# Releasing loads behind TensorE's steps and queueing one-hot rows by step, in windowed attention with a sticky mixture of experts

## The chip, the cores and the metric

The kernel runs on 1 core of one Trainium2 chip. The metric is the device time of one execution in microseconds (us). A profile is one further execution, taken with the hardware profiler; its trace gives every instruction a start and a duration. TensorE (PE) multiplies matrices and transposes, VectorE (DVE) and ScalarE (ACT) work on PSUM and SBUF, GpSimd (Pool) does masked copies and indirect gathers, and SyncE (SP) issues most of the transfers. PE, SP, ACT and Pool each follow their own program in order.

## The reference

Eight batches of eight heads: 512 local and 32 global tokens, head width 64, all in float32. A local token attends to the 32 global tokens and to local tokens at most 32 away; a global token attends to all 544. The result, one row of 512 numbers per token, goes through a mixture of 8 experts of which each token uses one. The choice is sticky:

```
s_l = concat([q_l @ k_g, where(|i - j| <= 32, q_l @ k_l, -1e9)]) / 8 ; out_l = softmax(s_l) @ [v_g, v_l]
out_g = softmax(q_g @ [k_g, k_l] / 8) @ [v_g, v_l]
x = [out_g, out_l] with the heads side by side            # (8, 544, 512)
logits = x @ w_gate ; gate = sigmoid(x @ w_local)
for each batch, for s in order:
    e = argmax(logits[s]) if s == 0 or gate[s] < 0.5 else the expert of token s - 1
    out[s] = softmax(logits[s])[e] * (relu(x[s] @ w1[e]) @ w2[e])     # w1: 512x1024, w2: 1024x512
```

## The kernel before

**Attention.** Class Attn works in 48 steps (`run`, from L427). A batch has six: l0, l1, g0, l2, g1, l3. An l step is a pair of heads of local queries, a g step the global queries of two pairs. Step s makes the scores of unit s and, for the unit of two steps before, the transposes and the products with v. On PE an l step is: transposes of the older unit (L264, or L332 after a global unit), the mask written into two PSUM score banks (L236), a piece of transposing finished rows for the router (L356), 32 score matmuls in two banks of 16 (L247), and 64 small products with v (L280, or 48 at L343 for a global unit). A g step has its scores at L300. DVE takes maxima and subtracts them bank by bank (L252, L254), ACT takes exponentials (L258) and copies transposes out of PSUM (L266, L333).

**Operands.** One q and k load per pair (`load`, L178, 528 KB) fills one of four buffers, `raw`; one v load per pair (`loadv`, L188, 1040 KB) fills one of four `v` buffers; a batch has one load of the global queries (L182). All are issued by SP in program order, each l step asking for q and k two pairs ahead and then for v one pair ahead. An issue waits only for its buffer to be free. Pool copies q and k into the layout of the scores (`prep`, L191: `qbd` in two selects, `kx` in four; two buffers of each), one pair ahead of the scores.

**Router.** The routing of finished batches is written as generators (`gens`). `drip` takes a few of their instructions at a time and puts them between DVE's maximum and subtraction, so they run amid attention: keys (L741 in `keys`), probabilities (L769 in `probs`), then `f4`, which stores the batch's rows to a scratch table in DRAM: the local rows from ACT's queue (L420, 1056 KB), the global ones in four transfers from SP (L424), and their numbers from ACT (L425). After the fifth batch `stage_a` ranks the tokens of the first five batches, and `low` makes 21 one-hot tiles of 128x128 (L916), one Pool instruction each, in a run of 3 tiles per turn of the generator. `pick` then has 21 matmuls of these tiles with `oe` on PE (L1013), whose sums give the rows that the first three blocks of the mixture gather. Nothing else uses these tiles until later lists are made.

**Mixture.** Weights come in pieces of 512 KB (L1154); ACT rounds each into a high part (L1164), and DVE, or Pool for the first two, subtracts it to get a low part (L1174). Three products of high and low parts stand for one in float32. `mm1` (L1265) multiplies a block of 256 tokens by w1, ACT and DVE make the high and low parts of the result (L1267, L1268), and `mm2` (L1276) multiplies by w2. PSUM has eight banks, `ps[0]` to `ps[7]`: attention's score banks are `ps[0]` to `ps[2]`, and the router's transposes (L356) use `ps[3]`. The mixture's ring `ph` of results of `mm1` starts with `ps[2]`, then `ps[3]`. Its first block begins before attention has ended: the last two units' transposes and products, and the last batches' routing, are put between its matmuls (`tail`, `hook`).

Of the kernel before, what the change touches and what calls it, by code (L numbers as in the profile page):

```python
# [18 lines left out]
P = 128  # L19
# [19 lines left out]
NX = 3  # L39
LISTS = "lists"  # L40
# [58 lines left out]
class Attn:  # L99
    def __init__(self, tc, cst, tl, at1, at2, raw, ps, qk, qg, vw, xs):  # L100
# [29 lines left out]
        self.cur = {}  # L130
        self.gens = []
# [40 lines left out]
    def load(self, b, pr):  # L172
        nc = self.nc
        if pr == 0:
            self.cur[b] = {"v": []}
        c = self.cur[b]
        t = c[("qk", pr)] = self.ld()
        nc.sync.dma_start(t, self.qk[b, pr])  # L178
# [5 lines left out]
    def loadv(self, b, pr):  # L184
        nc = self.nc
        v = self.v()
        self.cur[b]["v"].append(v)
        nc.sync.dma_start(v.rearrange("p w c -> p (w c)"), self.vw[b, pr])  # L188
# [49 lines left out]
    def l_s(self, st, hb):  # L238
# [4 lines left out]
        for t in range(4):  # L243
            for t2 in range(2):
                w = 8 * hb + 2 * t + t2
                f = 32 * (3 * (w // 2) + w % 2)
                nc.tensor.matmul(sp[64 * t2:64 * t2 + 64, t], qbd[:, w], kf[:, f:f + P], start=False, stop=True, skip_group_check=True)  # L247
# [12 lines left out]
    def l_t(self, st, hb):  # L260
        nc = self.nc
        tp = self.bank(self.ps_t)
        for i in range(4):
            nc.tensor.transpose(tp[:, i], st["pe"][:, 4 * hb + i], self.cst.idf)  # L264
# [61 lines left out]
    def g_t(self, st):  # L326
        nc = self.nc
        pt = st["pt"] = self.ptg()
        for c0 in (0, 3):
            tp = self.bank(self.ps_t)  # L330
            for i in range(3):
                nc.tensor.transpose(tp[:, i], st["pg"][:, c0 + i], self.cst.idf)  # L332
# [80 lines left out]
    def f4(self, b, rt):  # L413
# [6 lines left out]
        nc.scalar.dma_start(self.xs[r0:r0 + 4 * P].rearrange("(t p) r -> p t r", p=P), xa)  # L420
# [4 lines left out]
        nc.scalar.dma_start(xsg[:, DM:ROW], rt.gx[rq])  # L425

    def run(self, rt, moe):  # L427
# [29 lines left out]
        for s in range(n):  # L457
# [4 lines left out]
            sg = st is not None and not sl  # L462
            if nl:
                if npr + 2 < len(pairs):
                    b, i = pairs[npr + 2]["u"]
                    self.load(b, i)
                    if i == 0:
                        self.load_g(b)
                if npr + 1 < len(pairs):
                    self.loadv(*pairs[npr + 1]["u"])  # L470
                npr += 1
                if npr < len(pairs):
                    self.prep(pairs[npr])
            if sl:
                self.l_t(st, 0)
                self.l_t(st, 1)
            if sg:
                self.g_t(st)
            if nl:
# [5 lines left out]
            if nl:  # L485
                self.l_s(nx, 0)
                self.l_max(nx, 0)
# [111 lines left out]
class Route:  # L599
# [186 lines left out]
    def stage_a(self, pk, po):  # L786
# [11 lines left out]
        for c0 in range(0, CA, 3):  # L798
            yield from self.low(c0, min(c0 + 3, CA), True)
# [194 lines left out]
    def pick(self, cid, phi, o2, c0, c1, i0, groups, po, wait=2):  # L994
# [14 lines left out]
        yield from lag(wait)  # L1009
        yield PSUM  # L1010
# [74 lines left out]
class Moe:  # L1085
    def __init__(self, tc, cst, rt, xs, buf, raw, ps, w1, w2, out):
# [14 lines left out]
        self.ph, self.py, self.xtp = Ring(ps[2:4]), Ring(ps[0:2]), Ring(ps[4:6])  # L1101
# [68 lines left out]
    def flush(self):  # L1170
        nc = self.nc
        while self.pend:
            pool, raw, hi, lo = self.pend.pop(0)
            (nc.gpsimd if pool else nc.vector).tensor_tensor(out=lo, in0=raw, in1=hi.bitcast(F32), op=ALU.subtract)  # L1174
# [326 lines left out]
def kernel(ctx: ExitStack, tc: tile.TileContext, qk, qg, vw, wgl, wgg, w1, w2, out):  # L1501
# [23 lines left out]
    at.at1, at.at2 = s1, s2  # L1525
    at.run(rt, moe)
# [57 lines left out]
```

## Time and profile before

| | before |
|---|---|
| median of 3 runs | 692.18 us (690.45 to 694.25) |
| the profiled execution, its own time | 690.5 us |
| its span | 688.8 us |
| mean granted TensorE clock | 0.984 |
| PE busy | 659.1 us, 96% |
| DVE busy | 425.9 us, 62% |
| ACT busy | 343.0 us, 50% |
| Pool busy | 212.0 us, 31% |
| scores of local pairs (L247) | 1024 matmuls, 65.9 us |
| moved by the DMA engines | 151.45 MB, 220 GB/s |

The span is the time from the first to the last instruction in the trace; the execution's own time is 1.7 us longer. Attention takes about the first 240 us, the mixture the rest. In rows of the trace "out<-in" names the tiles that an instruction writes and reads, xN counts instructions, and what stands in brackets behind a row is the idle time of the engine before it and what ended it. In groups of waits the columns are the total in us, how many times, and the longest.

### The profile page before, as it was taken

The page shows a single profiled execution, that of the slowest core. Times are in us where ns is not written, and L with a number is a line of the kernel's source. Part 1 is how long each engine was busy: PE and PEld are TensorE (multiplying, and loading weights), DVE is VectorE, ACT ScalarE, POOL GpSimd, SP SyncE. Part 2 cuts the span into 40 slices and gives each one's busy share as a digit, 9 for nine tenths or more (in the row PEclk, how much of TensorE's full clock was granted, in tenths as well). Part 3 has the DMA queues.
Part 4 walks back from the last instruction along what each step waited for, and adds up shares of the span by engine and source line. Part 5 has one row for each costly group of instructions (what it writes and reads, how often), then busy time and mean ns, then how long its engine had stood idle before and what let it go on. Part 6 is the DMA issues. An engine that isn't in the chain of part 4 may idle for free.

```text
span 688.8 us, 18451 instructions
## 1 busy us (share of the span) xinstructions
PE 659.1 (96%) x7253; PEld 566.6 (82%) x7253; DVE 425.9 (62%) x1050; ACT 343.0 (50%) x614; POOL 212.0 (31%) x342
## 2 busy tenths in 40 slices
PE   8999999999979799998998999999999999999995
PEld 7788788877767788887887988889898889888994
DVE  7878787777877777994517636325354516255573
ACT  4565565664646474653326635344444325255563
POOL 7734434343674211132022403040403020133023
PEclk9999999999999899999998999999999999999998
DMA  8957977979576486878319547347466417265673
GB/s 334 362 210 258 335 257 276 346 279 332 177 285 227 158 309 234 264 247 277 125 60 320 196 161 244 101 130 230 149 213 194 146 57 230 68 227 177 226 272 103
DMA packets 43012, 151.45 MB, mean 220 GB/s; under 512 B 7965, under 2 KB 9245, under 8 KB 38688
## 3 DMA queue, kind: packets, MB, share of 16 engines
q1 hardware_dynamic: 30928, 118.25, 49.4%
q0 software_dynamic: 6960, 21.90, 9.6%
q10 hardware_dynamic: 4896, 8.80, 3.5%
q8 instruction: 78, 1.28, 0.8%
q14 instruction: 150, 1.23, 0.6%
HBM read 130.55 MB, written 19.69 MB: 218 GB/s over the span
## 4 chain that ended last, share of the span: by engine, by line
PE 80%; DVE 10%; POOL 4%; issue 4%; ACT 1%; POOLq 0%; ACTq 0%; DVEq 0%
PE ps L1276 27%; PE ps L1265 25%; PE ps L247 7%; PE ps L264 4%; PE ps L280 3%; PE ps L1219 3%; PE ps L300 2%; POOL o L916 2%; PE ps L356 2%; PE ps L343 2%; DVE wp L1174 2%; PE ps L332 1%; DVE wq L1174 1%; PE ps L371 1%; PE ps L236 1%
## 5 line engine op out<-in xcount | busy, mean ns | idle before, releaser
L1282 POOL DMA_INDIRECT out_dram<-y,tk x39 | 42.9, 1100 | 315.1 <-ACT y L1281 232.7
L1276 PE MATMUL ps<-wp,wq 128*128 128x512 f32 x504 | 129.5, 404 | 1.0 <-ACT wq L1379 1.0
L1276 PEld LDWEIGHTS ps<-wp,wq 128*128 128x128 f32 x504 | 94.1, 192 | 21.3 <-ACT wq L1379 1.3
L1265 PE MATMUL ps<-wp,wp 128*128 128x256 f32 (+5 forms) x672 | 109.3, 322 | 0.3 <-issue 0.3
L1265 PEld LDWEIGHTS ps<-wp,wp 128*128 128x128 f32 x672 | 103.6, 188 | 5.3 <-issue 0.4
L1268 DVE SCALAR_TENSOR_TENSOR wq<-ps,wq 128x256 fp32r<-128x256 f32 (+5 forms) x80 | 41.7, 525 | 73.8 <-ACT wq L1267 66.4
L1267 ACT ACTIVATE wq<-ps 128x256 fp32r<-128x256 f32 (+5 forms) x80 | 37.3, 469 | 79.1 <-PE ps L1265 69.4
L1222 DVE TENSOR_TENSOR wp<-ps,wp 128x512 fp32r<-128x512 f32 x40 | 27.6, 691 | 78.3 <-ACT wp L1221 78.2
L191 POOL TENSOR_SCALAR_AFFINE_SELECT qbd<-raw 64x512 f32<-64x512 f32 x62 | 44.4, 715 | 89.1 <-PE ps L247 69.7
L247 PE MATMUL ps<-kx,qbd 128*64 128x128 f32 x1024 | 65.9, 280 | 3.9 <-POOL kx L191 3.5
L247 PEld LDWEIGHTS ps<-kx,qbd 128*64 128x64 f32 x1024 | 56.6, 139 | 11.8 <-POOL kx L191 6.7
L1281 ACT ACTIVATE y<-ps,pp 128x512 f32<-128x512 f32 x39 | 26.9, 689 | 77.7 <-PE ps L1276 70.7
L252 DVE TENSOR_REDUCE mx<-ps 128x4 f32<-128x512 f32 x64 | 43.8, 685 | 32.0 <-PE ps L247 32.0
L258 ACT ACTIVATE pe<-pe 128x512 f32<-128x512 f32 x64 | 40.8, 638 | 43.3 <-DVE pe L254 43.3
L1174 DVE TENSOR_TENSOR wp<-raw,wp 128x1024 fp32r<-128x1024 f32 x47 | 56.9, 1217 | 2.9 <-ACT wp L1164 2.8
L1205 POOL DMA_INDIRECT xa<-xs,idx x42 | 52.3, 1245 | 16.3 <-issue 10.0
L1164 ACT CAST wp<-raw 128x1024 fp32r<-128x1024 f32 x49 | 50.9, 1047 | 2.7 <-DVE f L930 1.5
L1221 ACT CAST wp<-ps 128x512 fp32r<-128x512 f32 x40 | 23.4, 588 | 53.2 <-PE ps L1219 53.2
L254 DVE TENSOR_TENSOR pe<-ps,mx 128x512 f32<-128x512 f32 x64 | 43.9, 686 | 1.0
L191 POOL TENSOR_SCALAR_AFFINE_SELECT kx<-raw 128x384 f32<-128x384 f32 (+3 forms) x127 | 43.2, 373 | 2.9 <-DMA raw<-in_qk_dram 0.8
L266 ACT COPY pt<-ps 128x512 f32<-128x512 f32 x64 | 34.7, 600 | 9.8 <-PE ps L264 9.1
L280 PEld LDWEIGHTS ps<-v,pt 128*32 128x32 f32 x2048 | 32.0, 110 | 9.2 <-issue 6.5
(280 smaller groups left out, 1182.5 us busy)
## 6 DMA issues: line engine op xcount, KB each, us to landing
raw<-in_w_dram SPq DMA_DIRECT2D x78, 512.0 KB, 4.3
v<-in_vw_dram SPq DMA_DIRECT2D x32, 1040.0 KB, 7.9
raw<-in_qk_dram SPq DMA_DIRECT2D x32, 528.0 KB, 7.5
xa<-in_w_dram SPq DMA_DIRECT2D x26, 512.0 KB, 4.7
xT<-in_w_dram SPq DMA_DIRECT2D x20, 512.0 KB, 5.3
xs<-xa ACTq DMA_DIRECT2D x8, 1056.0 KB, 8.6
qgb<-in_qg_dram SPq DMA_DIRECT2D x8, 128.0 KB, 5.0
xa<-xs,idx POOLq DMA_INDIRECT x42, 4.9
```

What stands on the lines that cost most here:

```text
L191: self.nc.gpsimd.affine_select(out=out, in_=in_, pattern=pat, compare_op=ALU.is_ge, fill=0.0, base=0, channel_multiplier=0)
L247: nc.tensor.matmul(sp[64 * t2:64 * t2 + 64, t], qbd[:, w], kf[:, f:f + P], start=False, stop=True, skip_group_check=True)
L252: nc.vector.tensor_reduce(out=mx, in_=st["sps"][hb], axis=AX.X, op=ALU.max)
L254: nc.vector.tensor_tensor(out=st["pe"][:, 4 * hb:4 * hb + 4], in0=st["sps"][hb], in1=mx.broadcast_to([P, 4, P]), op=ALU.subtract)
L280: nc.tensor.matmul(o[32 * w4:32 * w4 + 32, g, h], pt[:, 2 * g + w4 // 2, w4 % 2, h, :], v[:, w, h * (D + 1):(h + 1) * (D + 1)], start=True ...
L1164: nc.scalar.copy(out=hi, in_=raw)
L1174: (nc.gpsimd if pool else nc.vector).tensor_tensor(out=lo, in0=raw, in1=hi.bitcast(F32), op=ALU.subtract)
L1205: self.nc.gpsimd.indirect_dma_start(out=self.xr[j] if k == "early" else self.xr4[:, j], out_offset=None, in_=src, in_offset=bass.IndirectO ...
L1265: nc.tensor.matmul(ph, a[:, dc, fs], b_[:, dc, n0:n1], start=(n == 0), stop=(n == 11))
L1268: nc.vector.scalar_tensor_tensor(out=hl[:, fc, n0:n1], in0=ph, scalar=0.0, in1=hh[:, fc, n0:n1].bitcast(F32), op0=ALU.max, op1=ALU.subtract)
L1276: nc.tensor.matmul(py, a[:, fc, js], b_[:, fs], start=(fc == 0 and k == 0), stop=(fc == 7 and k == 2))
L1282: sc = nc.gpsimd.indirect_dma_start(out=self.out, out_offset=bass.IndirectOffsetOnAxis(ap=self.g[1][:, j:j + 1], axis=0), in_=y, in_offset ...
```

## The change

There are five parts.

1. `get` issues q, k and v loads with a dependency besides the buffer's. An l step emits its v load behind its transposes, and it depends on the last of them; q and k (and behind them the global queries, which have no such dependency) are emitted behind the first score bank and depend on its last matmul, except in step 0. SP's order turns from q and k, then v, to v, then q and k.
2. Of the 21 one-hot tiles the first 6 are made by DVE, in two instructions of 3 tiles; the other 15 are put into a list `pq` of five turns of 3 Pool instructions. An l step takes one turn, behind its `prep`; a g step takes two. `pick` goes on only once the list is empty.
3. The last batch's stores of local rows and of its numbers are issued by SP.
4. The ring `ph` starts with `ps[3]`, then `ps[2]`.
5. Pool's split of a weight piece is four instructions of 256 columns.

The core of the diff:

```
+CD = 6
...
+        self.gate = self.last = None
+        self.pq = []
...
         t = c[("qk", pr)] = self.ld()
-        nc.sync.dma_start(t, self.qk[b, pr])
+        self.get(t, self.qk[b, pr])
...
-        nc.sync.dma_start(v.rearrange("p w c -> p (w c)"), self.vw[b, pr])
+        self.get(v.rearrange("p w c -> p (w c)"), self.vw[b, pr])
+
+    def get(self, out, in_):
+        d = self.nc.sync.dma_start(out, in_)
+        if self.gate is not None:
+            self.tc.add_manual_dep(d.ins, self.gate.ins.name, mybir.DependencyInfo(mybir.DependencyClass.Sync, mybir.DependencyReason.DATA), reason="pace")
...
-        nc.scalar.dma_start(self.xs[r0:r0 + 4 * P].rearrange("(t p) r -> p t r", p=P), xa)
+        q = nc.scalar if b < B - 1 else nc.sync
+        q.dma_start(self.xs[r0:r0 + 4 * P].rearrange("(t p) r -> p t r", p=P), xa)
...
-        nc.scalar.dma_start(xsg[:, DM:ROW], rt.gx[rq])
+        q.dma_start(xsg[:, DM:ROW], rt.gx[rq])
...
+            ahead = pairs[npr + 1:npr + 3] if nl else []
             if nl:
-                if npr + 2 < len(pairs):
-                    b, i = pairs[npr + 2]["u"]
-                    self.load(b, i)
-                    if i == 0:
-                        self.load_g(b)
-                if npr + 1 < len(pairs):
-                    self.loadv(*pairs[npr + 1]["u"])
                 npr += 1
                 if npr < len(pairs):
                     self.prep(pairs[npr])
+            for _ in range(2 - nl):
+                if self.pq:
+                    self.pq.pop(0)()
...
+            self.gate = self.last
+            if ahead:
+                self.loadv(*ahead[0]["u"])
...
                 self.l_s(nx, 0)
+                self.gate = self.last if s > 0 else None
+                if len(ahead) > 1:
+                    b, i = ahead[1]["u"]
+                    self.load(b, i)
+                    if i == 0:
+                        self.load_g(b)
                 self.l_max(nx, 0)
...
-        for c0 in range(0, CA, 3):
-            yield from self.low(c0, min(c0 + 3, CA), True)
+        for c0 in range(0, CD, 3):
+            yield from self.low(c0, c0 + 3, False)
+        for c0 in range(CD, CA, 3):
+            self.pq.append(lambda c0=c0: all_(self.low(c0, min(c0 + 3, CA), True)))
...
+        while self.pq:
+            yield
         yield PSUM
         lp = po()
...
-        self.ph, self.py, self.xtp = Ring(ps[2:4]), Ring(ps[0:2]), Ring(ps[4:6])
+        self.ph, self.py, self.xtp = Ring([ps[3], ps[2]]), Ring(ps[0:2]), Ring(ps[4:6])
...
-            (nc.gpsimd if pool else nc.vector).tensor_tensor(out=lo, in0=raw, in1=hi.bitcast(F32), op=ALU.subtract)
+            m = 4 if pool else 1
+            for k in range(m):
+                f = slice(1024 // m * k, 1024 // m * (k + 1))
+                (nc.gpsimd if pool else nc.vector).tensor_tensor(out=lo[:, f], in0=raw[:, f], in1=hi[:, f].bitcast(F32), op=ALU.subtract)
```

Line numbers move: L178 and L188 become L192 (both in `get`), L191 L197, L247 L253, L264 L270, L420 L427, L424 L431, L741 L754, L916 L931, L1013 L1030, L1174 L1194, L1265 L1285.

On PE, from the second score bank of the last batch's l1 (kx_147, qbd_145), before; `ps` are PSUM banks, `o` the one-hot tiles, `pe` the exponentials:

```order
L247 MATMUL ps_63<-kx_147,qbd_145 64x128 x8
L280 MATMUL ps_70<-v_136,pt_142 32x65 x16
L280 MATMUL ps_69<-v_136,pt_143 32x65 x16
L264 MATMUL ps_68<-idf,pe_138 128x128 x4
L264 MATMUL ps_67<-idf,pe_138 128x128 x4
L363 MATMUL ps_66<-idf,xg_111 128x128
L300 MATMUL ps_64<-raw_77,qgb_153 64x256
L300 MATMUL ps_64<-raw_78,qgb_153 64x256
L300 MATMUL ps_65<-raw_77,qgb_153 64x288
L300 MATMUL ps_65<-raw_78,qgb_153 64x288
L1013 LDWEIGHTS o_290
L1013 MATMUL ps_70<-oe,o_290 128x12
```

The same place after, from the mask of that unit; the one-hot matmuls' first, and their last with what follows:

```order
L242 MATMUL ps_65<-mask,idb 128x4x2x32
L242 LDWEIGHTS idb
L242 MATMUL ps_63<-mask,idb 128x4x2x32
L362 MATMUL ps_66<-idf,xa_108 128x128 x4
L253 MATMUL ps_65<-kx_147,qbd_145 64x128 x8
L1030 LDWEIGHTS o_290
...
L1030 MATMUL ps_70<-oe,o_290 128x12
L253 MATMUL ps_63<-kx_147,qbd_145 64x128 x8
L286 MATMUL ps_69<-v_136,pt_142 32x65 x16
L286 MATMUL ps_70<-v_136,pt_143 32x65 x16
```

The 21 matmuls moved from behind the scores of g0 to between the two score banks of l1. The last six of them (tiles 15 to 20) wait for Pool's last turn.

On Pool, the one-hot tiles amid the preparations, before: raw_80 is the last pair of the seventh batch, raw_77 and raw_78 the first two of the last.

```order
L916 TENSOR_SCALAR o_290<-io_261,plo 128x128 x12
L191 AFFINE_SELECT qbd_145<-raw_80 64x16x32 x2
L191 AFFINE_SELECT kx_147<-raw_80 128x128
L191 AFFINE_SELECT kx_147<-raw_80 128x6x64
L191 AFFINE_SELECT kx_147<-raw_80 128x32
L191 AFFINE_SELECT kx_147<-raw_80 128x7x32
L916 TENSOR_SCALAR o_290<-io_261,plo 128x128 x9
L191 AFFINE_SELECT qbd_144<-raw_77 64x16x32 x2
```

After, from the first pair of the last batch to its third (raw_79):

```order
L931 TENSOR_SCALAR o_290<-io_261,plo 128x128 x6
L197 AFFINE_SELECT qbd_144<-raw_77 64x16x32 x2
...
L931 TENSOR_SCALAR o_290<-io_261,plo 128x128 x3
L197 AFFINE_SELECT qbd_145<-raw_78 64x16x32 x2
...
L931 TENSOR_SCALAR o_290<-io_261,plo 128x128 x3
L197 AFFINE_SELECT qbd_144<-raw_79 64x16x32 x2
...
L931 TENSOR_SCALAR o_290<-io_261,plo 128x128 x3
```

Nine tiles stood ahead of the first pair's preparation; six do now, and the last three turns stand ahead of the second pair, ahead of the third, and behind the third.

On SP, the loads of the end of one batch and the start of the next in mid-attention (raw_79 and raw_80 are third and fourth pairs, raw_77 a first), before, with the semaphores that each waits for:

```order
L178 DMA raw_79<-in_qk_dram 128x1056 [waits DMAHW1_49,Pool_49]
L188 DMA v_134<-in_vw_dram 128x2080 [waits DMAHW3_49,PE_49]
L178 DMA raw_80<-in_qk_dram 128x1056 [waits DMAHW5_49,Pool_49]
L188 DMA v_135<-in_vw_dram 128x2080 [waits DMAHW6_49,PE_49]
L178 DMA raw_77<-in_qk_dram 128x1056 [waits DMAHW7_49,PE_49,Pool_49]
```

After:

```order
L192 DMA v_134<-in_vw_dram 128x2080 [waits DMAHW2_49,PE_49]
L192 DMA raw_79<-in_qk_dram 128x1056 [waits DMAHW4_49,PE_49,Pool_49]
L192 DMA v_135<-in_vw_dram 128x2080 [waits DMAHW5_49,PE_49]
L192 DMA raw_80<-in_qk_dram 128x1056 [waits DMAHW6_49,PE_49,Pool_49]
L192 DMA v_136<-in_vw_dram 128x2080 [waits DMAHW7_49,PE_49]
```

Each v load stands ahead of its step's q and k, and every q and k load waits for PE.

More of the change, by code (lines that the diff above doesn't have):

```diff
@@ L172, in load @@
     def load(self, b, pr):
-        nc = self.nc
         if pr == 0:
@@ L184, in loadv @@
     def loadv(self, b, pr):
-        nc = self.nc
         v = self.v()
         self.cur[b]["v"].append(v)
-        nc.sync.dma_start(v.rearrange("p w c -> p (w c)"), self.vw[b, pr])
+        self.get(v.rearrange("p w c -> p (w c)"), self.vw[b, pr])
[3 more added lines that the diff above has]
+            self.tc.add_manual_dep(d.ins, self.gate.ins.name, mybir.DependencyInfo(mybir.DependencyClass.Sync, mybir.DependencyReason.DATA), reason="pace")
     def cp(self, out, in_, pat):
@@ L246, in l_s @@
                 f = 32 * (3 * (w // 2) + w % 2)
-                nc.tensor.matmul(sp[64 * t2:64 * t2 + 64, t], qbd[:, w], kf[:, f:f + P], start=False, stop=True, skip_group_check=True)
+                self.last = nc.tensor.matmul(sp[64 * t2:64 * t2 + 64, t], qbd[:, w], kf[:, f:f + P], start=False, stop=True, skip_group_check=True)
     def l_max(self, st, hb):
@@ L263, in l_t @@
         for i in range(4):
-            nc.tensor.transpose(tp[:, i], st["pe"][:, 4 * hb + i], self.cst.idf)
+            self.last = nc.tensor.transpose(tp[:, i], st["pe"][:, 4 * hb + i], self.cst.idf)
         pt = self.pt()
@@ L331, in g_t @@
             for i in range(3):
-                nc.tensor.transpose(tp[:, i], st["pg"][:, c0 + i], self.cst.idf)
+                self.last = nc.tensor.transpose(tp[:, i], st["pg"][:, c0 + i], self.cst.idf)
             nc.scalar.copy(out=pt[:, c0:c0 + 3], in_=tp[:, 0:3])
@@ L1525 @@
     at.at1, at.at2 = s1, s2
+    rt.pq = at.pq
     at.run(rt, moe)
```

## The prediction

> **What bounds the kernel now.** I read the page's busy times, stretches of 20 to 26 us (start and end; length; busy time and instructions of PE, PEld, DVE, ACT, POOL; granted clock; DMA share; GB/s), then what PE waited for in the first 345 us.
>
> ```profile
> span 688.8 us, 18451 instructions
> 10.00:30.00 20.00, 19.06 (x413) 15.43 (x411) 16.69 (x58) 12.44 (x29) 13.74 (x44) 1.00 1.01 396
> 90.00:110.00 20.00, 20.00 (x429) 16.30 (x427) 16.36 (x59) 12.61 (x32) 7.21 (x17) 1.00 0.82 287
> 190.00:210.00 20.00, 16.16 (x377) 13.66 (x366) 16.16 (x62) 8.75 (x20) 12.48 (x25) 0.91 0.82 295
> 210.00:236.00 26.00, 22.06 (x387) 19.16 (x386) 20.17 (x60) 13.42 (x30) 10.64 (x12) 0.87 0.51 176
> PE ps L1265 <- DVE pe L254: 3.7, 1, 3.7
> PE ps L247 <- POOL kx L191: 3.5, 2, 2.9
> PE ps L343 <- issue: 2.8, 3, 1.2
> PE ps L264 <- issue: 1.3, 2, 0.8
> PE ps L356 <- issue: 0.7, 1, 0.7
> PE ps L247 <- issue: 0.3, 1, 0.3
> ```
>
> A wait row gives the total, how often, and the longest. TensorE sets the time: busy 20.00 of 20 us in mid-attention. It loses time in two places, before 210 us (16.16 of 20, clock 0.91) and before 236 us (22.06 of 26, clock 0.87), by one wait of 3.5 us for Pool and one of 3.7 for DVE. Another 2.8 + 1.3 + 0.7 + 0.3 = 5.1 us is idle with no releaser. The change touches all three.
>
> **1. The Pool stall goes (-5.4).** Pool's and PE's rows in order of time, and the stretch after the stall:
>
> ```profile
> 187.97 5.24 POOL L916 TENSOR_SCALAR o<-io,plo 128x128 bf16<-128x128 bf16 x9
> 193.16 1.49 POOL L191 TENSOR_SCALAR_AFFINE_SELECT qbd<-raw 64x512 f32<-64x512 f32 x2
> 194.73 1.50 POOL L191 TENSOR_SCALAR_AFFINE_SELECT kx<-raw 128x128 f32<-128x128 f32 x4
> 195.24 0.44 PE L247 MATMUL ps<-kx,qbd 128*64 128x128 f32 x4 [2.94 <-POOL kx L191]
> 196.28 3.25 PE L247 MATMUL ps<-kx,qbd 128*64 128x128 f32 x28 [0.60 <-POOL kx L191]
> 196.08:199.49 3.41, 3.21 (x32) 2.88 (x33) 1.62 (x4) 0.00 (x0) 2.89 (x7) 0.50 0.87 334
> 201.96 1.97 PE L247 MATMUL ps<-kx,qbd 128*64 128x128 f32 x32
> ```
>
> Nine one-hot rows (0.58 us each) stand ahead of the last batch's first qbd and kx; PE waits 2.94 + 0.60, and the clock is then 0.50 for 3.41 us, in which half is lost: 1.7. With three rows a step this preparation starts over 5 us earlier. I count 2.94 + 0.60 + 1.7 and 0.2 of pipeline gap: -5.4.
>
> **2. A new wait stands 1.3 steps later (+7.1).** The one-hot matmuls (L1013, L1030 after) come only once Pool's queue list is empty, which puts them between the two score banks of the last batch's second pair. Matmuls 16 to 21 read Pool's last three rows, and those stand behind the preparation of the third pair, whose q and k load is now held until the first pair's first bank.
>
> ```profile
> 78.04 1.90 PE ps L247 x32
> 86.85 1.90 PE ps L247 x32
> 76.36 1.02 PE ps L264 x8
> DMA to landing us min/median/max: 4.8/7.9/11.4
> DMA to landing us min/median/max: 3.6/7.5/12.2
> 207.18 0.67 PE L1013 MATMUL ps<-oe,o 128*128 128x12 bf16 x21
> 193.14 0.37 ACTq L420 DMA_DIRECT2D xs<-xa  x1
> ```
>
> The first two rows are score starts two steps apart: 8.81, so 4.41 a step. The landings are v's, then q and k's. Without stall 1 PE reaches the new place about 197.5 (201.96, plus 0.95 for half of those 32 matmuls, less 5.4). Pool's line, in before's time: the second pair's load opens behind the fourth pair's first bank of the batch ahead, near 188.6 (two steps of 4.41 before 201.96 less stall 1, plus 0.95), lands 4.5 later (0.9 above the fastest), and its preparation takes 3.0 by rows 193.16 and 194.73, to 196.1; three rows take 1.75, to 197.85; the third pair's preparation 3.0 again, to 200.85; three rows more, to 202.6. So PE waits 5.1 even if the third load is no limit. With that load opened a step later, at 193.0, and landing after 7.5 (the median; the store of the activations, issued at 193.14 before, shares the DMA engines) it is 193.0 + 7.5 + 3.0 + 1.75 = 205.25: a wait of 7.75. I take 5.5, nearer the lower end, because with loads spread out a landing nearer the fastest is likely. After the shorter wait above the clock cost 1.7, and it could fall through two such stretches: 0.5 to 3.4, taken 1.9. The place that L1013 left, where DVE's sums held PE for some 0.3, gives that back. Together +7.1 (5.3 to 10.9). Behind the waiting matmul stand the second bank, and with it DVE's subtract and ACT's exponentials.
>
> **3. Loads held back (+0.7, and +1.0 at the start).** By the chain rows a third pair's scores follow the first's by 8.81. v's gate opens after the transposes (76.36 + 1.02 = 77.38); the fastest v landing puts it at 82.18, q and k's 528 KB behind it take 1.37 at 396 GB/s, to 83.55, preparation 3.0, to 86.55; PE wants it at 86.85. So 0.3 us are to spare once in each of 7 batches, and the median landings would miss it.
>
> ```profile
> SPq L188 <- PE ps L343: 103.5, 14, 9.4
> 11.02 1.50 POOL L191 TENSOR_SCALAR_AFFINE_SELECT qbd<-raw 64x512 f32<-64x512 f32 x2 [1.21 <-DVE mx L252]
> 15.39 1.97 PE L247 MATMUL ps<-kx,qbd 128*64 128x128 f32 x32
> ```
>
> SyncE already waited 103.5 us for PE to free v buffers, so the queue was paced before; the hold binds q and k, whose early issue goes. I take +0.7: most fit, some miss by little. Below it is 0; above it 7.7, worked out under the rival Slower. At the start v's second load now goes ahead of q and k of the third pair, in a stretch at 396 GB/s: 1040 KB take 2.7 us. The preparation at 11.02 ends 3.0 later, 1.4 ahead of the scores at 15.39; 2.7 later it would be 1.3 late: +1.0, since it did not start at its landing but at DVE's release (0 to 1.3).
>
> **4. End of attention (-3.9).** DVE, Pool, PE and ACT in order of time, the 0.50 stretch, and the same DVE operation elsewhere:
>
> ```profile
> 222.53 3.03 DVE L741 TENSOR_TENSOR leq<-leq,ro 128x40 f32<-128x40 f32 x1
> 256.39 0.20 DVE L741 TENSOR_TENSOR leq<-leq,ro 128x40 f32<-128x40 f32 x1
> 223.14 2.36 POOL L1174 TENSOR_TENSOR wp<-raw,wp 128x1024 fp32r<-128x1024 f32 x1
> 229.49 2.06 DVE L769 TENSOR_SCALAR lsu<-lsu 128x5 f32<-128x5 f32 x1
> 191.17 0.32 DVE L769 TENSOR_SCALAR lsu<-lsu 128x5 f32<-128x5 f32 x1
> 229.16 2.36 POOL L1174 TENSOR_TENSOR wp<-raw,wp 128x1024 fp32r<-128x1024 f32 x1 [3.67 <-ACT wp L1164]
> 227.54 2.07 PE L1265 MATMUL ps<-xh,wp 128*128 128x256 f32 x8 [3.74 <-DVE pe L254]
> 226.80:233.62 6.82, 6.08 (x28) 6.08 (x29) 5.31 (x20) 1.90 (x5) 2.36 (x1) 0.50 0.32 106
> 232.42 0.43 ACTq L420 DMA_DIRECT2D xs<-xa  x1
> 233.45 0.38 ACT L1267 ACTIVATE hh<-ps 128x256 fp32r<-128x256 f32 x1 [4.23 <-DVE gx L783]
> 234.26 0.93 PE L343 MATMUL ps<-v,ptg 128*32 128x65 f32 x48 [0.20 <-ACT ptg L333]
> ```
>
> L741 takes 0.20 alone and 3.03 when it overlaps Pool's split, ending with it (225.56, 225.50); L769 likewise ends at 231.55 with the second (231.52), but took 0.32 amid Pool's stream of 0.58 us rows. In pieces of 0.6 the two lose at most one piece each: 3.03 - 0.6 + 2.06 - 0.6 = 3.9 comes out of DVE's line. The other score bank frees PE from L254, so the 3.74 stall goes. What is late next is ACT: the sixth batch's stores (L420) wait for DVE, and hh and the global transposes' copy stand behind them, releasing PE at 234.26. That chain moves up by DVE's 3.9: PE at 230.4. I take -3.9; at best 3.74 + 1.9 = -5.6, if full clock holds; if pieces follow without a gap, 0.
>
> The Trainium skill, "SBUF — State Buffer", section "Who interferes with whom", says that a DVE instruction with two SBUF inputs and a Pool one exclude each other, the later waiting for the whole instruction. L741 agrees (3.03 against 0.20). Taken strictly it speaks against this change: the one-hot tiles moved to DVE have two SBUF inputs and meet Pool's selects, and each would wait for one select and then take its own time, 1.1 together; were none of it covered, the sum would be 2.2 worse and 0.5 in place of -1.7. Here it is covered, as point 5 works out from DVE's idle share.
>
> **5. The rest (-1.2).** The unexplained 5.1 us depend on where instruction fetches fall among the queues' traffic; spread loads may ease them: -1.0 (-5.1 to +3, as others may appear). The last stores leave ACT: two issues of 0.4 us, -0.2 (-1.5 to 0). Two one-hot operations on DVE:
>
> ```profile
> 288.07 2.02 DVE L919 TENSOR_TENSOR o<-io,plo 128x640 bf16<-128x640 bf16 x3
> ```
>
> Three of five tiles cost 0.67, so one of three tiles 0.4, inside DVE's idle 3.6 of 20 us: 0 (to +0.8).
>
> **The sum.** -5.4 + 7.1 + 0.7 + 1.0 - 3.9 - 1.2 = -1.7. The profiled execution takes 690.5 (span 688.8), so 688.8 in its like; the runs' median is 1.7 above it, at 692.18, so I forecast 690.5 against that median. A measurement can tell 0.5% (3.5 us) from no change.
>
> **The rivals.**
> *Faster.* The end of attention yields its whole 5.6 (1.7 more than taken) and the fetch stalls go altogether (4.1 more): -1.7 - 5.8 = -7.5, 684.7. For it: both are idle time on the bounding engine. Against: stalls without a releaser need not follow the loads. Chance 0.31.
> *The hold never binds.* SyncE's 103.5 us of waiting would be the true pace; q and k of the third pair come as early as before, then the third pair's preparation starts when kx's buffer is free, at the end of the first pair's scores, 201.96 + 1.97 - 5.4 - 4.41 = 194.1, and the last rows end 3.0 + 1.75 later, at 198.9. The wait shrinks to 1.4 with no clock loss, 1.1 in place of 7.1: -7.7, 684.5. Against: the order shows a wait on PE's newest step at every q and k load, and v's buffers alone were what it waited for before. Chance 0.05.
> *Slower.* The held q and k land after the point: PE then waits for kx in each batch's run of three adjoining pairs. It decides when the landing passes 83.85 in the chain above, 4.9 after the first bank's release at 78.99; the median landing of 7.5 says it does, by 2.6, the bare transfer says not. A landing of 6.0, inside the upper half of 3.6 to 7.5, misses by 1.1, and 7 x 1.1 = 7.7 replaces 0.7: +5.3, 697.5; with wait 2 at its end as well, +9.1, 701.3. Chance 0.26.
>
> **How the numbers follow.** My forecast has 0.38, the rivals 0.31, 0.05 and 0.26. Range 683 to 700: it takes in both faster cases with 1.5 to spare and the slower one short of its far end; the forecast's own range is 688.7 to 695.6. Faster 0.31 + 0.05 = 0.36, same 0.38, slower 0.26.
>
> **What would show it.** Right: no wait for kx near 193 us; one wait of 4 to 7 us at L1030 for Pool, with a 0.50 stretch behind it; L741 below 0.9; first L1285 without a stall. Wrong: a wait below 2 us at L1030, waits for kx in most batches, or fetch stalls far from 5 us.

## The result and the profile after

The changed kernel takes 701.36 us (median of 4 runs, 696.91 to 703.67) against 691.69 us (4 runs, 690.45 to 694.25): 1.0116 times the time before, 95% interval 1.0083 to 1.0150. It is slower by 9.7 us, outside the range that was forecast. The profiled execution has a span of 699.0 us against 688.8, 10.2 more.

The page of the changed kernel, and what PE waited for in its first 345 us (total, times, longest):

```profile
span 699.0 us, 18469 instructions
PE ps L1030 <- POOL o L931: 6.8, 3, 6.0
PE ps L286 <- issue: 4.1, 5, 2.1
PE ps L349 <- ACT ptg L339: 2.7, 1, 2.7
PE ps L253 <- POOL kx L197: 1.8, 4, 0.6
PE ps L242 <- DVE leq L752: 1.8, 1, 1.8
```

The two waits that bounded the kernel before are gone: the 3.5 us for Pool at the last batch's first pair (the 1.8 us left are four other waits, all before the seventh batch) and the 3.7 us at the mixture's first block. A wait at L1030 that did not exist, 4.1 us without a releaser at L286 and a wait for ACT stand in their place.

Where the 10.2 us come from is read from PE's rows in order of time. These four start a pair's scores: the first pair of the seventh batch and its last pair, each before and after.

```profile
162.54 0.66 PE L247 MATMUL ps<-kx,qbd 128*64 128x128 f32 x8
187.62 2.17 PE L247 MATMUL ps<-kx,qbd 128*64 128x128 f32 x32
```

```profile
167.52 0.66 PE L253 MATMUL ps<-kx,qbd 128*64 128x128 f32 x8
195.42 1.97 PE L253 MATMUL ps<-kx,qbd 128*64 128x128 f32 x32
```

PE is 5.0 us late at the seventh batch, before any one-hot row is made, and 7.8 late at that batch's last pair. Then the rows of the last batch's first pairs and of the place of L1030:

```profile
199.83 1.97 PE L253 MATMUL ps<-kx,qbd 128*64 128x128 f32 x32
204.83 1.09 PE L253 MATMUL ps<-kx,qbd 128*64 128x128 f32 x16
212.45 0.19 PE L1030 MATMUL ps<-oe,o 128*128 128x12 bf16 x1 [5.99 <-POOL o L931]
213.73 1.97 PE L253 MATMUL ps<-kx,qbd 128*64 128x128 f32 x16
215.63 2.21 PE L286 MATMUL ps<-v,pt 128*32 128x65 f32 x64
213.60:217.00 3.40, 3.39 (x63) 2.96 (x64) 2.14 (x5) 0.63 (x1) 2.19 (x3) 0.50 0.19 40
233.37 1.97 PE L253 MATMUL ps<-kx,qbd 128*64 128x128 f32 x32
```

The second pair's scores start at 204.83, against 201.96 before: only 2.9 late, so the stall for Pool that went gave back 4.9. After L1030 the same 16 matmuls take 1.97 that took 1.09, and 64 products with v 2.21 in place of 1.12: the stretch from 213.60 to 217.00 has a granted clock of 0.50. The last pair starts at 233.37 against 220.78, 12.6 late. From there to the end 2.4 are won back: 12.6 - 2.4 = 10.2.

Why L1030 waited is in Pool's rows:

```profile
200.33 1.50 POOL L197 TENSOR_SCALAR_AFFINE_SELECT qbd<-raw 64x512 f32<-64x512 f32 x2 [5.06 <-DMA raw<-in_qk_dram]
203.40 1.77 POOL L931 TENSOR_SCALAR o<-io,plo 128x128 bf16<-128x128 bf16 x3
208.91 1.50 POOL L197 TENSOR_SCALAR_AFFINE_SELECT qbd<-raw 64x512 f32<-64x512 f32 x2 [3.74 <-DMA raw<-in_qk_dram]
211.79 1.76 POOL L931 TENSOR_SCALAR o<-io,plo 128x128 bf16<-128x128 bf16 x3
```

Pool sits idle for 3.74 us until the third pair's q and k land, prepares them, and only then makes the three rows that PE has been waiting for since 206.46.

The end of attention: DVE, PE and ACT.

```profile
235.12 0.19 DVE L754 TENSOR_TENSOR leq<-leq,ro 128x40 f32<-128x40 f32 x1
240.43 0.65 DVE L788 TENSOR_TENSOR gx<-lpr,lsu 32x8 f32<-32x8 f32 x1
241.09 0.68 DVE L791 COPY xa<-tok 128x4 int32<-128x4 int32 x1
243.63 0.93 PE L349 MATMUL ps<-v,ptg 128*32 128x65 f32 x48 [2.67 <-ACT ptg L339]
```

The DVE operation of 3.03 us takes 0.19. From the last pair's first score to L349 it is 10.3 us (243.63 - 233.37) where it was 13.5 (234.26 - 220.78).

### The profile page after: what moved, and what is told of

Its sections match the earlier page's. It is cut to its first block, busy times and chain, and to the rows that moved or that the text cites. A ratio compares the mean times of both kernels' runs of the same rounds, so it can differ in the third digit from the quotient of the medians.

```text
span 699.0 us, 18469 instructions
## 1 busy us (share of the span) xinstructions
PE 658.2 (94%) x7253; PEld 564.1 (81%) x7253; DVE 423.4 (61%) x1052; ACT 343.0 (49%) x614; POOL 209.0 (30%) x342
## 4 chain that ended last, share of the span: by engine, by line
PE 55%; DVE 6%; issue 1%; ACT 1%; SPq 1%; DMA 1%; POOL 0%; POOLq 0%; DVEq 0%; ACTq 0%
PE ps L1296 26%; PE ps L1285 25%; PE ps L1239 2%; DVE wp L1194 1%; DVE wq L1194 1%; SPq L431 1%; DMA raw<-in_w_dram 1%; PE ps L1408 0%; DVE xl L1194 0%; DVE xT L1020 0%; DVE xT L1018 0%; DVE o L934 0%; POOL xa L1225 0%; ACT wp L1181 0%; DVE xl L1242 0%
## 5 line engine op out<-in xcount | busy, mean ns | idle before, releaser
L1302 POOL DMA_INDIRECT out_dram<-y,tk x39 | 41.5, 1064 | 314.0 <-ACT y L1301 233.1
L1296 PE MATMUL ps<-wp,wq 128*128 128x512 f32 x504 | 127.0, 398 | 1.0 <-ACT wq L1399 1.0
L1285 PE MATMUL ps<-wp,wp 128*128 128x256 f32 (+5 forms) x672 | 109.3, 322 | 1.0 <-issue 1.0
L1296 PEld LDWEIGHTS ps<-wp,wq 128*128 128x128 f32 x504 | 92.4, 188 | 20.7 <-ACT wq L1399 1.2
L1285 PEld LDWEIGHTS ps<-wp,wp 128*128 128x128 f32 x672 | 103.6, 188 | 6.0 <-issue 1.1
L197 POOL TENSOR_SCALAR_AFFINE_SELECT qbd<-raw 64x512 f32<-64x512 f32 x62 | 44.5, 718 | 110.2 <-DMA raw<-in_qk_dram 81.1
L253 PE MATMUL ps<-kx,qbd 128*64 128x128 f32 x1024 | 66.1, 279 | 2.1 <-POOL kx L197 1.8
L253 PEld LDWEIGHTS ps<-kx,qbd 128*64 128x64 f32 x1024 | 55.9, 138 | 10.6 <-POOL kx L197 5.3
L264 ACT ACTIVATE pe<-pe 128x512 f32<-128x512 f32 x64 | 40.8, 638 | 47.5 <-DVE pe L260 47.5
L1194 DVE TENSOR_TENSOR wp<-raw,wp 128x1024 fp32r<-128x1024 f32 x47 | 56.8, 1216 | 2.8 <-ACT wp L1181 2.8
L197 POOL TENSOR_SCALAR_AFFINE_SELECT kx<-raw 128x384 f32<-128x384 f32 (+3 forms) x127 | 43.7, 377 | 3.1 <-DMA raw<-in_qk_dram 1.0
L286 PEld LDWEIGHTS ps<-v,pt 128*32 128x32 f32 x2048 | 32.8, 111 | 14.0 <-issue 11.5
L286 PE MATMUL ps<-v,pt 128*32 128x65 f32 x2048 | 38.5, 223 | 4.8 <-issue 4.1
```

The costliest lines, as they stand in the source:

```text
L197: self.nc.gpsimd.affine_select(out=out, in_=in_, pattern=pat, compare_op=ALU.is_ge, fill=0.0, base=0, channel_multiplier=0)
L253: self.last = nc.tensor.matmul(sp[64 * t2:64 * t2 + 64, t], qbd[:, w], kf[:, f:f + P], start=False, stop=True, skip_group_check=True)
L286: nc.tensor.matmul(o[32 * w4:32 * w4 + 32, g, h], pt[:, 2 * g + w4 // 2, w4 % 2, h, :], v[:, w, h * (D + 1):(h + 1) * (D + 1)], start=True ...
L1194: (nc.gpsimd if pool else nc.vector).tensor_tensor(out=lo[:, f], in0=raw[:, f], in1=hi[:, f].bitcast(F32), op=ALU.subtract)
L1285: nc.tensor.matmul(ph, a[:, dc, fs], b_[:, dc, n0:n1], start=(n == 0), stop=(n == 11))
L1296: nc.tensor.matmul(py, a[:, fc, js], b_[:, fs], start=(fc == 0 and k == 0), stop=(fc == 7 and k == 2))
```

## The experiments

The times are medians; "before" is the kernel before on the same chip in the same session, and the ratio is to that, with its 95% interval. A gain or a loss given in us below is its ratio's share of that time. The parts are those of the change.

| run | what it is | us | before | ratio |
|---|---|---|---|---|
| pace_only | part 1 | 697.7 | 693.0 | 1.0080 (1.0052 to 1.0109) |
| rows_only | part 2 | 690.5 | 693.0 | 0.9972 (0.9947 to 0.9997) |
| end_only | parts 4, 5 | 690.4 | 693.0 | 0.9968 (0.9943 to 0.9992) |
| no_hold | all, no added dependency | 690.7 | 693.0 | 0.9972 (0.9953 to 0.9992) |
| no_pace | all but part 1 | 688.5 | 693.2 | 0.9937 (0.9914 to 0.9960) |
| order_only | part 1's order, no dependency | 690.8 | 693.2 | 0.9973 (0.9957 to 0.9989) |
| pace_early | part 1, q and k with v | 697.5 | 693.2 | 1.0060 (1.0035 to 1.0084) |
| rows_first | all, rows ahead of preparation | 695.5 | 693.2 | 1.0039 (1.0020 to 1.0058) |
| hold_v | part 1, v alone held | 698.0 | 692.6 | 1.0073 (1.0046 to 1.0101) |
| hold_qk | part 1, q and k alone held | 693.2 | 692.6 | 1.0012 (0.9988 to 1.0035) |
| hv_prev | hold_v, a step earlier | 691.8 | 692.3 | 0.9988 (0.9959 to 1.0018) |
| hv_late | hold_v, 1.7 us later | 706.1 | 692.3 | 1.0183 (1.0130 to 1.0236) |
| hv_l01 | hold_v, steps l0, l1 | 694.6 | 692.3 | 1.0031 (0.9996 to 1.0066) |
| hv_l23 | hold_v, steps l2, l3 | 695.6 | 692.3 | 1.0037 (1.0003 to 1.0071) |
| no_pace_sp | no_pace, seventh batch's stores by SP | 685.2 | 692.6 | 0.9904 (0.9870 to 0.9938) |
| order_rows_sp | no_hold, rows_first, those stores by SP | 682.9 | 692.6 | 0.9866 (0.9835 to 0.9896) |

**One part at a time.** Each of the first three is the kernel before with the named part of the diff; the fourth takes the dependency out of the changed kernel:

```
     def get(self, out, in_):
-        d = self.nc.sync.dma_start(out, in_)
-        if self.gate is not None:
-            self.tc.add_manual_dep(d.ins, self.gate.ins.name, mybir.DependencyInfo(mybir.DependencyClass.Sync, mybir.DependencyReason.DATA), reason="pace")
+        self.nc.sync.dma_start(out, in_)
```

> The kernel before with part 1 alone: each v load held until its step's transposes are done and placed ahead of q and k, which are held until the first score bank. Theory H (the held loads cost the time, since they come in bursts behind which q and k and TensorE's instruction fetches land late): slower by 4 to 6 us, as attention up to the sixth batch is 5 us longer in the changed kernel's profile, and the waits of PE without a releaser sum to 7 us or more against 5.1 before. Theory R (the queue of one-hot rows costs the time by itself): within 1 us of before.

> The kernel before with part 2 alone: six one-hot tiles on DVE, the other fifteen queued by step, the pick behind the empty queue; loads issued as before. Theory H: the wait at the one-hot matmuls came from the held third q and k load, so here it is 0 to 1.5 us, the Pool stall of 3.5 us with its half clock is gone, and the time falls by 4 to 6 us. Theory R: the matmuls still wait 5 to 7 us for Pool's last rows and then run at half clock, and the time rises by 3 to 4 us.

> The kernel before with parts 4 and 5 alone: the mixture's first PSUM bank is not a score bank, and Pool's two weight splits are four pieces each. Both theories: faster by 2 to 4 us, the DVE operation at the end of attention (3.03 us before) at 0.2 to 0.9, the first block of the mixture without its 3.74 us wait; the wait that is left is for ACT's copy of the global transposes, behind the sixth batch's stores. If the whole of it is hidden behind those stores, within 1 us.

> The changed kernel without the added dependencies; the order of the issues (v, then q and k behind the first bank's instructions) stays. Theory H: faster than before by 6 to 8 us (the Pool stall's 4.9 and the end's 2.4 gained, little lost), so 8 to 10 us under the changed kernel less what the start costs. Theory R: 1 to 2 us slower than before (3.8 of the rows less 2.4 of the end). If SyncE's own place in the order paces the loads as much as the added dependency does, the time is that of the changed kernel.

Part 1 alone costs 0.80%, 5.5 us; the rows and the end alone each gain about 0.3%. So the held loads carry the loss and the queue of rows is no loss by itself: the theory that the rows cost the time falls. Part 3 has no run of its own. The rows' gain is smaller than the 4 to 6 us expected of them. What PE waited for in the run of the rows alone, from 180 us on, and then in the run without the hold:

```profile
PE ps L347 <- ACT ptg L337: 3.3, 2, 3.0
PE ps L1280 <- DVE pe L258: 3.1, 1, 3.1
```

```profile
PE ps L1028 <- POOL o L929: 4.0, 3, 3.2
PE ps L347 <- ACT ptg L337: 3.2, 2, 2.7
```

With before's loads the one-hot matmuls wait for nothing, and PE only comes earlier to the end of attention, where it waits 3.1 us more for ACT (3.3 against 0.2). Without the hold but in part 1's order, they still wait 4.0. SP issues the second pair's q and k at 186.41, behind a v load that waited for its buffer until 185.99, and the third pair's only at 192.91, when the second pair's have landed; the last rows stand behind the third pair's. This wait, with the slower matmuls behind it, is about what no_hold missed of its 6 to 8 us: order_rows_sp, which lacks it, is 7.3 us faster, some 2.3 of them by its other change (no_pace to no_pace_sp).

**Without part 1, and what of part 1 costs.** no_pace undoes part 1 in the changed kernel; order_only takes the dependency out of pace_only; pace_early issues q and k right behind v, held by the same transposes; rows_first moves the turn on Pool:

```
+            for _ in range(2 - nl):
+                if self.pq:
+                    self.pq.pop(0)()
             if nl:
                 npr += 1
                 if npr < len(pairs):
                     self.prep(pairs[npr])
-            for _ in range(2 - nl):
-                if self.pq:
-                    self.pq.pop(0)()
```

> The changed kernel without part 1: loads issued in before's order and with buffers' waits alone; parts 2 to 5 stay. If part 1 carries the whole loss: the rows' 1.9 us and the end's 2.2 us, measured alone, add up, and the time is 4 us under before (0.4 to 0.8%). If the two gains overlap (both only move PE up to the wait for ACT's copy behind the sixth batch's stores): 2 us under before.

> The kernel before with part 1's order of issue but without its added dependencies: v behind the step's transposes, q and k behind the first bank's instructions, held by their buffers alone. Theory A (the added dependency is the cost, by opening q and k's load too late for Pool): within 1 us of before, no more waits for kx than before's two. Theory B (SyncE's order is the cost: q and k stand behind a v load that waits for its buffer): slower by 3 to 6 us like the run of part 1 alone.

> The kernel before with part 1, but q and k are issued right behind v and held by the same transposes, 1.7 us earlier than behind the first bank. If the lateness of q and k's landing is the cost (waits for kx of 0.3 to 0.7 and 0.6 us in the batches, 3.7 us over before's): these waits go and the time falls to 1 to 2 us over before. If the bursts' delay of TensorE's instruction fetches is the cost, the time stays 4 to 6 us over before, with waits without a releaser of 7 us.

> The changed kernel with each step's turn of one-hot rows ahead of its preparation on Pool and not behind it, so that the last three rows no longer stand behind the held third pair; loads held as in the changed kernel. If the wait at the one-hot matmuls costs what the profile shows (6.75 us and 2 of half clock): it falls to under 1.5 us, and the time is 6 to 9 us under the changed kernel, 0 to 2 us over before. If the wait only moves to the scores of the third pair, which need the same load: 0 to 3 us under the changed kernel.

no_pace is 4.4 us under before: the gains of the rows and the end add up once part 1 is out. From there to the changed kernel (0.9937 to 1.0116, in different sessions) part 1 costs 12.4 us, against 5.5 alone: the rest comes from its meeting with the other parts. order_only is not slower, so for the loads alone the dependency is the cost and not the order. pace_early stays 4.2 us over, though its waits for kx outside the old Pool stall are down to 0.6 us: most of the loss is not kx coming late. rows_first is 0.77% under the changed kernel (1.0039 against 1.0116, in different sessions), 5 us, less than the 6 to 9 expected. PE's rows there:

```profile
203.51 1.09 PE L253 MATMUL ps<-kx,qbd 128*64 128x128 f32 x16
204.54 0.68 PE L1030 MATMUL ps<-oe,o 128*128 128x12 bf16 x21
205.15 1.09 PE L253 MATMUL ps<-kx,qbd 128*64 128x128 f32 x16
```

All 21 matmuls run without a wait, and the second bank takes 1.09 us and not 1.97. That the last rows stood behind the held third pair is thereby shown to be the cause of the wait at L1030.

**Which hold.** hold_v is pace_only with the dependency taken from q and k:

```
-                self.gate = self.last if s > 0 else None
+                self.gate = None
```

hold_qk is pace_only with the dependency taken from v:

```
-            self.gate = self.last
+            self.gate = None
```

> The kernel before with part 1 where only the v loads are held (by the step's transposes); q and k keep part 1's order of issue and wait for their buffers. The run of part 1 without any hold was 2 us under before, with both holds 5.5 over. If the hold of v is what costs (v cannot start when its buffer comes free, and then v, q and k come in one burst): 3 to 5 us over before. If the hold of q and k is: within 2 us of before, and at most one wait for kx in the batches.

> The kernel before with part 1 where only q and k are held (by the first score bank); v waits for its buffer alone. If the hold of q and k is what costs: waits for kx in the batches as with both holds (3.7 us over before's), 4 to 6 us over before. If the hold of v is: 0 to 2 us over before, since v is then out of the way when q and k are released.

Against before, holding q and k costs nothing that can be told from 0 (1.0012, interval from 0.9988); holding v costs 0.73%, as much as both. The nearer comparison is with the same order of issue without a hold, order_only at 0.9973 in another session: by it the hold of q and k costs some 0.4% and that of v 1.0%. So v's hold is the larger cost, but that of q and k is not nothing. Four more runs vary the moment and the place of v's hold. hv_late issues v behind the first bank and holds it there. hv_prev keeps the dependency but on the transposes of the step before:

```
-            self.gate = self.last
+            self.gate, self.mark = self.mark, self.last
```

hv_l01 holds v at two of the four local steps, and hv_l23, with (2, 3), at the other two:

```
-            self.gate = self.last
+            self.gate = self.last if nx["u"][1] in (0, 1) else None
```

> As the run with v alone held, but v waits for the transposes of the step before, one step (4.4 us) earlier, so that the dependency is there and seldom binds. If the moment of release is what costs: the time falls to that of the order without a hold, 1 to 3 us under before. If the added dependency by itself costs (semaphore updates on PE or waits on SyncE): 4 to 6 us over before, as with the later release.

> As the run with v alone held, but v is issued behind the first score bank and held by it, 1.7 us later. If the moment of release costs, the loss grows: 6 to 9 us over before, with more waits for kx as q and k stand behind v. If not, it stays at 4 to 6.

> As the run with v alone held, but only at a batch's first two local steps. In before's trace these loads wait longest for their buffer anyway. If the hold costs where loads were issued back to back before, at the steps l2 and l3: at most 1 us over the order alone, 0 to 2 us under before. If it costs at the adjoining steps l0 and l1: 4 to 6 us over before.

> The complement: v held only at a batch's last two local steps (and the loads for the next batch's first pair with them). If the hold costs at l2 and l3: 4 to 6 us over before. If at l0 and l1: 0 to 2 us under before. If each of the two halves is 1 to 3 us over the order alone, the cost is spread over all steps.

The moment decides: 0.9988, 1.0073 and 1.0183 as v is released a step earlier, behind the transposes, and 1.7 us later. A dependency that seldom binds costs nothing that can be told: in hv_prev SP's waits for the transposes at L270 are 0.4 us in all, in hold_v 28 loads wait for transposes (113.8 us in 21 at L270, 19.6 in 7 at L338). The cost is not at one kind of step: each half of the loads is about 0.3% over before, at the edge of what can be told (intervals from 0.9996 and 1.0003), and 0.6% over order_only. With the late release PE waits for kx in each of the first six batches. Its waits from 16 to 165 us, which is attention up to the seventh batch:

```profile
PE ps L253 <- POOL kx L197: 9.4, 11, 1.8
PE ps L286 <- issue: 1.9, 1, 1.9
PE ps L349 <- issue: 1.5, 1, 1.5
```

Behind a v that is held stand q and k on SP's queue, so v's hold is also theirs, and the later it is, the more often Pool's preparation misses PE. Behind the transposes this happens little, and something else must carry the loss. The kernel of hold_v and that of order_only were therefore profiled a second time.

> A second profile of the run with v alone held by its step's transposes, to be read where its time is near its median of 698. If the loss is q and k landing late for Pool: waits for kx before the sixth batch's end of 2 to 4 us in 4 or more places (0.6 in the first look). If it is instruction fetches: waits without a releaser of 8 us or more over the same stretch (5.6 in the first look). If neither, TensorE's matmuls themselves take longer in that stretch.

> A second profile of the run with part 1's order and no hold, whose median was 690.8 and whose first profile was taken at 695.4. If its profile is near its median: waits without a releaser before the sixth batch's end of 2 to 4 us (5.5 in the first look), at most one wait for kx there.

The two executions took 696.4 and 690.6 us on the same chip (a run of before there took 695.6, above its usual, so only these two are compared). From 16 to 165 us PE waited, in hold_v's kernel and then in order_only's:

```profile
PE ps L286 <- issue: 2.3, 3, 1.0
PE ps L349 <- issue: 1.2, 1, 1.2
PE ps L362 <- issue: 1.0, 1, 1.0
PE ps L270 <- issue: 0.8, 1, 0.8
PE ps L253 <- issue: 0.8, 1, 0.8
PE ps L253 <- POOL kx L197: 0.8, 2, 0.4
```

```profile
PE ps L251 <- issue: 0.8, 1, 0.8
PE ps L251 <- POOL kx L195: 0.6, 1, 0.6
PE ps L284 <- issue: 0.5, 1, 0.5
```

Waits without a releaser are 6.1 us in the one and 1.3 in the other, waits for kx about the same. The seventh batch's scores start at 165.62 and 160.56:

```profile
165.62 0.55 PE L253 MATMUL ps<-kx,qbd 128*64 128x128 f32 x6
```

```profile
160.56 0.66 PE L251 MATMUL ps<-kx,qbd 128*64 128x128 f32 x8
```

Of these 5.1 us, 4.8 are waits without a releaser. The expectation's 8 us were too many and its partner's 2 to 4 too; the difference is what was looked for. It is not settled by these two, though: order_only's first profile had 5.5 us of such waits at 695.4 us, so they vary from one execution to the next by as much.

What these waits are, the records of the DMA queues show. Packets of 16 KB come on a queue that the profile calls instruction, 24 to 27 of them from 16 to 165 us, so some 6 us apart. In the twenty traces of these runs TensorE has 122 waits of 0.2 us or more without a releaser in that stretch, and every one ends between 1.0 and 1.7 us after such a packet has ended. They are fetches of instructions that came late. The longest in the changed kernel, and the packets from 41.5 to 42.6 us by queue:

```profile
43.77 0.31 PE L286 MATMUL ps<-v,pt 128*32 128x65 f32 x5 [2.07 <-issue]
q8 instruction: 1, 0.02, 5.5%
```

This packet starts at 41.54, just as the packets of the loads ahead of it come to an end. That loads delay the fetches in general, no run shows.

Over all profiles the waits do grow with v's hold. In the six whose v waits for its own step's transposes (the changed kernel, pace_only, pace_early, rows_first, hold_v twice) they are 5.6 to 7.7 us, 6.4 on average. In the six with part 1's order where v does not (order_only twice, no_hold, order_rows_sp, hold_qk, hv_prev) they are 1.3 to 5.5, 3.3 on average. That is 3 of the 7 us between hold_v and order_only. They are not the whole account: five kernels in before's order have 4.1 to 5.7 us of them, and none of these is slower than before.

**Beyond the two kernels.** no_pace_sp and order_rows_sp change one line more:

```
-        q = nc.scalar if b < B - 1 else nc.sync
+        q = nc.scalar if b < B - 2 else nc.sync
```

> The changed kernel without part 1, and with the seventh batch's stores (the sixth counted from zero) moved to SyncE like the last one's. If the wait for ACT's copy of the global transposes at the end of attention (2.7 us) stands behind these stores, it shrinks to 1 us or less, and the time falls 1 to 2.5 us further, to 6 us under before. If ACT is late by its own exponentials and casts, or the weights behind the stores on SyncE come late in their place, it stays at 4 us under before or rises.

> The changed kernel without the added dependencies but with part 1's order of issue, each turn of one-hot rows ahead of its step's preparation, and the seventh batch's stores on SyncE. Without holds, part 1's order alone was 2 us under before, but with the rows the one-hot matmuls still waited 4 us. If rows ahead of the preparation end that wait: 6 to 8 us under before, the fastest of all. If the order's gain is no more than the noise of placing instruction fetches: as the run without part 1 and with those stores moved.

Both beat before and the changed kernel; the fastest is order_rows_sp, 0.9866, 9.3 us under before, though its interval overlaps that of no_pace_sp. What ACT does at the end of attention in no_pace_sp:

```profile
226.13 0.23 ACT L772 ACTIVATE lpr<-lpr 128x40 f32<-128x40 f32 x1
226.29 0.38 ACT L1282 ACTIVATE hh<-ps 128x256 fp32r<-128x256 f32 x1
226.61 0.86 ACT L337 COPY ptg<-ps 128x384 f32<-128x384 f32 x2
```

No store stands between the probabilities and the copy, and PE's 2.7 us for that copy are gone. That the copy waited behind the seventh batch's stores is thereby shown.

## Why the prediction was wrong

The sum was -1.7 and the profile says +10.2. Of the 11.9 us between them 4.3 stand at the held loads and unexplained waits, 2.8 at the one-hot operations on DVE, 1.6 at the new wait, 1.5 at the end and 0.5 at the stall; 1.0 more come between the last batch's third and fourth pairs, for which the sum had no term, and 0.2 were forecast for the last stores and are not seen apart.

**Held loads (+0.7 and +1.0) and the unexplained waits (-1.0): here the prediction failed.** Together +0.7; up to the seventh batch it is +5.0. The step that failed reads "the hold binds q and k, whose early issue goes", and "spread loads may ease" the waits without a releaser. The runs show otherwise on both: the hold of v is the larger cost (0.73% over before and 1.0% over the same order without a hold, against 0.1% and 0.4% for q and k), and the waits without a releaser did not shrink. Up to the seventh batch they are 4.1 us at L286, shown above, and

```profile
PE ps L270 <- issue: 1.2, 1, 1.2
PE ps L349 <- issue: 0.8, 1, 0.8
PE ps L362 <- issue: 0.5, 1, 0.5
PE ps L253 <- issue: 0.3, 1, 0.3
```

In all 4.1 + 1.2 + 0.8 + 0.5 + 0.3 = 6.9 us, against 5.1. These 1.8 us and the 1.8 of waits for kx make 3.6 of the 5.0; the rest stands in neither. At the start the third pair's scores waited 0.2, not 1.0. The row that misled was SyncE's 103.5 us of waiting for v buffers: it was 14 waits, and there are 32 v loads. Four more waited, 5.7 us in all, and the rest were issued when SP came to them; with the hold 28 wait. For the waits without a releaser the prediction allowed up to 3 us more and took 1.0 less, and they came out on the side that it had not taken.

**The new wait (+7.1).** Right in place, cause and nearly in size: 6.8 us of waiting against 5.5, 2.0 of half clock against 1.9 (the two rows behind it take 1.97 - 1.09 and 2.21 - 1.12 longer), and 8.7 net from the second pair's scores to the third's. Nearer to the upper end, since the third load, issued at 201.00, kept Pool waiting until 208.91: 7.9 us, about the median of 7.5 and not near the fastest.

**The Pool stall (-5.4)** gave 4.9. The preparation did not start over 5 us earlier, as the working has it: with before's loads (rows_only) it is 2.8, at 190.39 against 193.16, and it then waits for PE's scores and not for rows. **The end (-3.9)** gave 2.4. DVE's L741 and L769 lost their long waits as worked out, but Pool's pieces took 0.73 and not 0.6, and one met nearly every operation of the chain that followed: L788 and L791 took 0.65 and 0.68. The prediction let the pieces hit two operations in all, and nearly each of them hit one. What is left is the wait of 2.67 for ACT's copy, behind the seventh batch's stores (the sixth of the prediction, which counts from zero).

**Two one-hot operations on DVE (0).** Wrong: they took 0.54 and 0.79 and not 0.4 each, and in the step after the rows DVE ran late enough for PE's mask to wait 1.8 for ACT's global exponentials, which wait for DVE's L316 (the row names L752, which ended in the same moment). This is most of the 2.8 us between the seventh batch's first and last pairs. It is 0.8 or 0.9 in rows_only, no_hold and no_pace_sp too, so it belongs to part 2; why it is 1.8 here is not shown, since it is 1.0 with the hold in rows_first and 1.3 without it in order_rows_sp. The two operations are not all that moved: since the generator no longer stops for Pool's turns, eleven list operations (L948 to L997, some 3.4 us) now run ahead of L316, from 188.40 on, where in before they came behind it, from 193.93 on. No run separates the two. The prediction had weighed what the Trainium skill says in "SBUF — State Buffer", section "Who interferes with whom": a DVE instruction with two SBUF inputs and a Pool instruction that reads SBUF exclude each other. Here the two took 1.33 together, between the 0.8 of the sum and the 2.2 of the strict reading. That the strict sum, 0.5 and not -1.7, came out nearer to +10.2 is luck.

```profile
185.23 0.79 DVE L934 TENSOR_TENSOR o<-io,plo 128x384 bf16<-128x384 bf16 x1
194.11 1.32 ACT L324 ACTIVATE pg<-ps,nb 128x192 f32<-128x192 f32 x5 [3.64 <-DVE nb L316]
194.78 0.27 PE L242 MATMUL ps<-mask,idb 128*128 128x256 bf16 x1 [1.77 <-DVE leq L752]
```

**The rivals.** "Slower" had the sign and about the size (697.5, up to 701.3), by a mechanism that was a small part of it: late q and k made 1.8 us of waits, not 7.7, so its size was luck. "Faster" failed in both its terms: the end gave 2.4 and not 5.6, and the fetch stalls did not go; even without part 1 the other parts gain 4.4 (no_pace) and not 7.5. That the hold never binds is refuted: 28 loads wait for it in hold_v. The signs named for a right forecast all came (no wait for kx near 193 us, 6.8 us at L1030 with a clock of 0.50 behind it, L741's 0.19, no stall at the first L1285); none of them looked at v's release.

What stays open: how v's hold costs all of its time. Shown is that the moment of v's release sets the loss and that late instruction fetches grow with the hold and carry some 3 of the 7 us. Why the fetches come late is only argued (from the loads' traffic), they vary between executions of one kernel, and the rest stands in no wait read here. In hv_late they do not grow; there it is kx.

## What to carry to other kernels

A load that is held until a step's own work is done needs all of its landing, and whatever stands behind it on the same queue, to fit into the steps that are left: try the same dependency one step earlier first, since here that turned a loss of 0.7% into none. Before work is queued behind a per-step preparation on an in-order engine, ask what the preparation waits for: three rows of 1.8 us were 6 us late because they stood behind a load. And count the waits of a row against the number of instructions that could have waited: here 14 long waits and 4 short ones of 32 loads left 14 that a new dependency could still delay.

## What was unexpected of the hardware

Cutting a Pool operation that reads SBUF into four made it dearer, 2.85 us in place of 2.36 (0.73 a piece and not 0.59), and spread DVE's loss over more operations: two of 3.03 and 2.06 before; after it 0.43 for L782 and, of the operations that followed, 0.47, 0.65 and 0.68 where the same ones took 0.18, 0.16 and 0.36 in before, from 192.27 to 192.99 us.

```profile
235.12 2.85 POOL L1194 TENSOR_TENSOR wp<-raw,wp 128x256 fp32r<-128x256 f32 x4
239.26 0.43 DVE L782 TENSOR_SCALAR lsu<-lsu 128x5 f32<-128x5 f32 x1
```
